# Another order of the first attention groups and of the first expert's tokens, filler products for TensorE, and fourteen subtractions on another engine

## The chip, the core and the metric

The program runs on one NeuronCore of a Trainium2 chip. Its engines are TensorE (PE; its weight loads are shown as PEld), VectorE (DVE), ScalarE (ACT), GpSimd (POOL) and SyncE (SP), which here issues the DMAs. Each engine works through its own instructions in order; semaphores tie them together. The metric is the device time of one launch in microseconds (us).

## What is computed

A block-windowed attention feeds a mixture of four experts without routing, and that feeds a gated MLP. Shapes: batch 2, 8 heads, 768 positions, head width 64, so 1536 tokens of width 512.

```python
k_sum = k.reshape(B, H, nb, 32, D).max(axis=3)       # 24 block maxima per head
v_sum = v.reshape(B, H, nb, 32, D).mean(axis=3)      # 24 block means per head
s_l = where(|i - j| < 16, scale * q @ k.T, -1e9)
s_s = scale * q @ k_sum.T + log(32)
a = softmax(concat([s_l, s_s]))
x = a @ concat([v, v_sum])                           # tokens x 512
p = domain_probs / (domain_probs.sum(-1) + 1e-9)
out = sum over e of p[:, e] * (relu(x @ w1[e]) @ w2[e])      # 512 -> 1024 -> 512, 4 experts
h = out @ w_in;  result = (h * sigmoid(1.702 * h)) @ w_out   # 512 -> 2048 -> 512
```

## The kernel before

**Numbers.** Matmuls take operands that are split into a high word (rounded to fp32r) and a low word (the rest, a subtraction). A product is a triple of matmuls: high by high, high by low, low by high. "Triple" below means these three.

**Attention groups.** A group is one batch, one head pair `hp` (two heads side by side on the 128 partitions) and four windows of 64 positions, 256 positions in all; there are 24 groups, numbered by the list `groups` (line 941). Batch 0 comes first: window start 0 for all four head pairs, then start 4, then start 8. A group passes through these steps, which the order below names by short words with the group's number: `Q`, `U` load queries and windowed values, `K`, `N` load keys and values of a head pair; `max` takes the 24 block maxima (DVE); for the first four groups `dl` and `dm` make the scores straight from keys and maxima (`direct_products`, L254), later ones copy windows (`win`, `wb`) and use `sc` (L247, 16 small matmuls); `msk` scales, masks and takes the row maximum (DVE, L276 and L281); `exp` is four exponentials with sums (ACT, L288) and adds 1e-9 to the sums (L292); `rec` inverts (DVE); `mul` scales (DVE `:v` or POOL `:g`, L300); `T` transposes (PE, L308); `aT` copies out (ACT, L314); `V` multiplies by the values (PE, L324); `xh` writes the high word of the result (ACT, L338), `low` the low word (DVE, L345). `mp`, `mq`, `mt`, `mc`, `mk`, `vb` make and spread the block means.

**First expert, batch 0.** `PIECES` (line 64) cuts its 768 tokens into pieces of 256 and 512, and the 8 blocks of 128 hidden columns make 16 units: 0 to 7 on the first 256 tokens, 8 to 15 on the other 512. Unit i has four first products, one for each head pair k (`f i.k`, L440; for units 0 to 3 they are called `e k.i` and have PSUM banks 0 to 3, later units share bank 4). Then `ga` applies relu and the gate (DVE, L392), `hh` makes the high word (ACT, L456), `hl` the low word (L398), and four second products `s i.d` (L478) add to the output banks. The gate values come from DRAM: `dp` loads, `gs`, `gr`, `gm` normalise, `ps` writes them to DRAM, `pb` reads them back spread over all partitions. The weights are loaded by `WA`, `WC`, split by `wh` (high, ACT) and `wl` (low, DVE or POOL).

**Pair 0.** The other experts and the MLP run in 44 pairs of hidden blocks by a seven-product scheme (`pair`); pair 0 is written out by hand at the end of the order. It needs sums over the tokens of batch 0: `wo` rebuilds x (DVE, L1033, four pieces), `d` are four differences (L490), `th`, `tl` their high and low words (L495, L498), `q` the seven products (L732), `mv`, `tt`, `tg`, `tr`, `tw` the way from them to the hidden words. `Sa`, `Ph`, `Pl` prepare the weights of pair 1.

**What sets the order.** The string `ORDER` lists all these steps; the loop under it records them in that order, so each engine gets its own steps in the order of the string. The tile pools and semaphores do the rest. Ahead of the string ten products of the identity with itself (L1139, "warm") keep PE working while the first loads land. The operands of the later stages (batch 1 of the experts, batch 0 and batch 1 of the MLP) come from `prepare`, which calls `operands` (L505): seven pieces, each a copy on ACT (L495) and a subtraction on POOL (L498, 128x768), and four differences on DVE. `spread` deals them out over pairs: the set "x" over pair 1 and pairs 9 to 11, the first set "y" over pairs 24 to 27, the second over pairs 29 to 31.

## Time and profile before

| what | value |
|---|---|
| median of 3 runs | 841.67 us (840.47 to 841.74) |
| the profiled execution's own time | 841.6 us |
| its span, first to last instruction | 839.8 us |
| PE busy | 824.9 us (98%) |
| DVE, ACT, POOL busy | 594.1, 418.5, 435.7 us |
| mean granted TensorE clock | 0.993 |

PE's busy time covers the modelled ends of pipelined matmuls, so a stretch that reads as busy can still run at half the clock or wait between instructions. The spacing of the starts tells more than the durations. From 152 us on the program is the regular sequence of pairs; what lies before is the stretch that the order string writes out.

### The profile page before, as it was taken

The page shows a single profiled execution, that of the slowest core. Times are in us where ns is not written, and L with a number is a line of the kernel's source. Part 1 is how long each engine was busy: PE and PEld are TensorE (multiplying, and loading weights), DVE is VectorE, ACT ScalarE, POOL GpSimd, SP SyncE. Part 2 cuts the span into 40 slices and gives each one's busy share as a digit, 9 for nine tenths or more (in the row PEclk, how much of TensorE's full clock was granted, in tenths as well). Part 3 has the DMA queues.
Part 4 walks back from the last instruction along what each step waited for, and adds up shares of the span by engine and source line. Part 5 has one row for each costly group of instructions (what it writes and reads, how often), then busy time and mean ns, then how long its engine had stood idle before and what let it go on. Part 6 is the DMA issues. An engine that isn't in the chain of part 4 may idle for free.

```text
span 839.8 us, 13639 instructions
## 1 busy us (share of the span) xinstructions
PE 824.9 (98%) x5114; PEld 747.3 (89%) x5114; DVE 594.1 (71%) x843; ACT 418.5 (50%) x972; POOL 435.7 (52%) x372
## 2 busy tenths in 40 slices
...
GB/s 289 203 174 186 114 65 211 115 218 285 218 289 206 162 228 185 223 285 290 233 289 280 255 278 101 54 73 150 151 204 178 170 199 201 247 167 116 171 78 76
DMA packets 48370, 159.93 MB, mean 190 GB/s; under 512 B 5424, under 2 KB 8752, under 8 KB 43184
## 3 DMA queue, kind: packets, MB, share of 16 engines
...
## 4 chain that ended last, share of the span: by engine, by line
PE 85%; DVE 8%; ACT 3%; issue 2%; DMA 2%; POOL 0%; DVEq 0%; POOLq 0%; ACTq 0%
PE o L856 25%; PE Y L732 19%; PE o L887 14%; PE X L732 5%; PE h L440 3%; PE o L478 3%; DVE S L602 2%; PE sc L247 2%; PE xo L324 2%; PE at L308 1%; DVE hid L398 1%; DVE g L774 1%; DMA k<-kq 1%; DVE x L1033 1%; PE warm L1139 1%
## 5 line engine op out<-in xcount | busy, mean ns | idle before, releaser
L856 PE MATMUL o<-hid,wB 128*128 128x512 f32 x1344 | 260.8, 336 | 0.7 <-POOL wB L642 0.6
L856 PEld LDWEIGHTS o<-hid,wB 128*128 128x128 f32 x1344 | 214.7, 188 | 22.0 <-POOL wB L642 1.0
L642 POOL TENSOR_TENSOR wB<-rawB,wB 128x512 fp32r<-128x512 f32 x88 | 122.9, 1407 | 158.0 <-ACT wB L638 148.7
L887 PE MATMUL o<-wB,hid 128*128 128x512 f32 x570 | 146.5, 394 | 0.3 <-ACT y L873 0.3
L784 ACT CAST hid<-g 128x384 fp32r<-128x384 f32 x172 | 88.3, 514 | 116.2 <-DVE g L774 84.8
L398 DVE TENSOR_TENSOR hid<-g,hid 128x384 fp32r<-128x384 f32 (+2 forms) x144 | 127.7, 899 | 6.8 <-ACT hid L784 5.3
L887 PEld LDWEIGHTS o<-wB,hid 128*128 128x128 f32 x570 | 105.7, 188 | 17.4 <-ACT y L873 0.7
L622 POOL TENSOR_TENSOR wA<-S,wA 128x512 fp32r<-128x512 f32 x48 | 72.6, 1513 | 37.0 <-ACT wA L618 26.8
L774 DVE SCALAR_TENSOR_TENSOR g<-g,pb 128x384 f32<-128x384 f32 x81 | 85.0, 1050 | 1.0
L622 POOL TENSOR_TENSOR wA<-rawA,wA 128x512 fp32r<-128x512 f32 (+1 forms) x48 | 56.5, 1179 | 48.7 <-ACT wA L618 39.8
L398 POOL TENSOR_TENSOR hid<-g,hid 128x384 fp32r<-128x384 f32 (+2 forms) x48 | 53.7, 1118 | 51.6 <-ACT hid L784 27.7
L732 PE MATMUL Y<-xt,wA 128*128 128x384 f32 x324 | 64.9, 334 | 0.0
L732 PE MATMUL Y<-xh,wA 128*128 128x384 f32 x216 | 63.7, 335 | 0.1
L797 ACT COPY prq<-Y 128x384 f32<-128x384 f32 x43 | 20.7, 480 | 80.7 <-PE Y L732 69.9
L695 POOL TENSOR_TENSOR arena<-arena 128x512 int32<-128x512 int32 x32 | 37.2, 1162 | 45.0 <-DVE arena L690 12.1
L732 PEld LDWEIGHTS Y<-xt,wA 128*128 128x128 f32 x324 | 53.9, 188 | 2.2
L638 ACT CAST wB<-rawB 128x512 fp32r<-128x512 f32 x88 | 52.5, 618 | 0.7 <-DMA rawB<-wts 0.7
L812 ACT COPY prq<-Y 128x384 f32<-128x384 f32 x43 | 20.6, 480 | 58.6 <-PE Y L732 58.6
L781 ACT ACTIVATE sg<-g 128x384 f32<-128x384 f32 x48 | 25.3, 527 | 48.5 <-DVE g L789 48.5
L782 DVE TENSOR_TENSOR g<-g,sg 128x384 f32<-128x384 f32 x48 | 37.0, 770 | 14.9 <-ACT sg L781 13.5
L789 DVE TENSOR_TENSOR g<-X,prq 128x384 f32<-128x384 f32 x43 | 23.8, 554 | 33.2 <-PE X L732 21.1
L602 DVE TENSOR_TENSOR S<-rawA 128x256 f32<-128x256 f32 x48 | 45.7, 954 | 1.8 <-POOL wA L622 1.8
...
## 6 DMA issues: line engine op xcount, KB each, us to landing
...
```

The lines of the kernel that those rows point to most:

```text
L398: engine.tensor_tensor(out=hl, in0=g, in1=hh.bitcast(F32), op=ALU.subtract)
L602: nc.vector.tensor_tensor(out=t[:, o], in0=a, in1=b, op=op)
L622: engine.tensor_tensor(out=lo, in0=x, in1=hi.bitcast(F32), op=ALU.subtract)
L638: nc.scalar.copy(wB[j][:, 0, f], rawB[j][:, f])
L642: nc.gpsimd.tensor_tensor(out=lo, in0=rawB[j][:, f], in1=hi.bitcast(F32), op=ALU.subtract)
L695: nc.gpsimd.tensor_tensor(out=o, in0=hi, in1=lo, op=ALU.add)
L732: nc.tensor.matmul(ps[:, 0:HS], ws[w], xs[x][:, k], start=(fresh and k == 0 and m == 0), stop=(k == 1 and m == 2), skip_group_check=True,)
L774: nc.vector.scalar_tensor_tensor(out=g, in0=g, scalar=0.0, in1=pbs[ph, s][:, tok], op0=ALU.max, op1=ALU.mult)
L782: nc.vector.tensor_tensor(out=g, in0=c, in1=sg, op=ALU.mult)
L784: heads.append(lambda: nc.scalar.copy(hh, g))
L856: nc.tensor.matmul(o, wB[j][:, w, f, c], tiles[f][:, x, t], start=fr, stop=last, skip_group_check=True,)
L887: nc.tensor.matmul(o, tiles[f][:, x, c], wB[j][:, w, f], start=(new and f == 1 and m == 0), stop=(stops and f == 0 and m == 2),)
```

## The change

1. The list of groups runs by head pair: for each head pair of batch 0 windows 0 and 4, then window 8 for all four. The first four groups, which make scores straight from the keys, are now head pairs 0 and 1 with two windows each. Their scores use PSUM banks 5, 3, 2 and 5 in place of bank 5 alone. The block means are spread by POOL for all groups but the first; for the other opening groups ACT writes one window's means and POOL three.
2. The first expert's tokens are cut into 512 and 256. The early first products of units 0 to 3 may be made by halves of 256 tokens (`e k.i.h`): for head pairs 0 and 1 by halves (16 triples of 256), for 2 and 3 whole (8 triples of 512).
3. Six warming products in place of ten, and twelve more (`x1`, on bank 1, which nothing else uses yet) between the first groups: six, two and four.
4. Adding 1e-9 to the sums is a step of its own, on ACT for 13 groups and on POOL for 11.
5. `prepare` takes an engine: the subtractions of the set "x" and of the first set "y" are on DVE, the second set "y" stays on POOL.
6. The order string is new throughout.

```diff
--- before.py
+++ after.py
@@ -36,6 +36,7 @@
 GQ = GW * WIN
 LAG = 2
 EARLY = 4
+WARM = 6
 NEG = -1.0e9
 
 TINY = math.ldexp(1.0 + 1.0 / 8, (897 << 20 >> 23) - 127)
@@ -61,7 +62,7 @@
         return psum.tile([P, 512], F32, tag=f"bank{n}", name=name)
 
 
-    PIECES = [(0, GQ), (GQ, S - GQ)]
+    PIECES = [(0, 2 * GQ), (2 * GQ, S - 2 * GQ)]
     units = [(c0, n, f) for c0, n in PIECES for f in range(NF)]
     N = len(units)
 
@@ -109,8 +110,8 @@
 
     def load_q(g):
         b, hp, w0 = g
-        if b == 0 and w0 == 0 and hp < HP - 1:
-            t = q_home[:, hp]
+        if g in groups[: HP - 1]:
+            t = q_home[:, groups.index(g)]
         else:
             t = att.tile([P, GQ], F32, tag="q", bufs=4, name="q{}{}{}".format(*g))
         c = PAD + w0 * WIN
@@ -227,9 +228,12 @@
         nc.tensor.transpose(ps[0:KA], vsum[hp % 2], ident)
 
     def spread_means(g):
-        nc.gpsimd.tensor_copy(
-            vs[g][KW:KA], vms[g[:2]][KW:KA].unsqueeze(1).to_broadcast([NB, GW, P])
-        )
+        b, hp, w0 = g
+        if b or w0 == 2 * GW:
+            out, means = vs[g][KW:KA], vms[b, hp][KW:KA]
+        else:
+            out, means = vs[g][KW:KA, 0 if w0 else 1 :], v_homes[hp // 2][KW:KA, hp % 2, 0]
+        nc.gpsimd.tensor_copy(out, means.unsqueeze(1).to_broadcast(list(out.shape)))
 
     def means_tile(b, hp):
         vms[b, hp] = att.tile([P, P], F32, tag="vm", bufs=4, name=f"vm{b}{hp}")
@@ -255,7 +259,7 @@
         b, hp, w0 = g
         k, q = kts[b, hp], qs[g]
         if c0 == 0:
-            scs[g] = bank(5, f"sc{b}{hp}{w0}")
+            scs[g] = bank({1: 3, 2: 2}.get(groups.index(g), 5), f"sc{b}{hp}{w0}")
         ps = scs[g]
         for j in range(GW):
             w = (w0 + j) * WIN
@@ -289,8 +293,16 @@
                 s[:, j, :], s[:, j, :], AF.Exp, bias=nm[:, j : j + 1], scale=1.0,
                 accum_out=sm[:, j : j + 1],
             )
-        nc.scalar.activation(sm, sm, AF.Copy, bias=1e-9)
         st[g] = (s, sm)
+
+    def tiny_term(g, e):
+        sm = st[g][1]
+        if e == "s":
+            nc.scalar.activation(sm, sm, AF.Copy, bias=1e-9)
+        else:
+            engines[e].tensor_scalar(
+                out=sm, in0=sm, scalar1=1.0, scalar2=1e-9, op0=ALU.mult, op1=ALU.add
+            )
 
     def inverses(g):
         nc.vector.reciprocal(out=st[g][1], in_=st[g][1])
@@ -432,14 +444,16 @@
             hid[i] = bank(hidden_bank(i), f"h{i}")
         products(i, k)
 
-    def products(i, k):
+    def products(i, k, h=None):
         c0, n, f = units[i]
-        c, x = slice(k * P, (k + 1) * P), slice(c0, c0 + n)
+        y0, y1 = (0, n) if h is None else (h * GQ, (h + 1) * GQ)
+        c, x = slice(k * P, (k + 1) * P), slice(c0 + y0, c0 + y1)
         whi, wlo = part_of(f, A, 0), part_of(f, A, 1)
         for m, (wt, xx) in enumerate(((whi, xh[0]), (whi, xl[0]), (wlo, xh[0]))):
             nc.tensor.matmul(
-                hid[i][:, 0:n], wt[:, c], xx[:, k, x],
-                start=(k == 0 and m == 0), stop=(k == KC - 1 and m == 2),
+                hid[i][:, y0:y1], wt[:, c], xx[:, k, x],
+                start=(k == 0 and m == 0 and not h), stop=(k == KC - 1 and m == 2),
+                skip_group_check=i < EARLY,
             )
 
     def gated_hidden(i):
@@ -448,10 +462,10 @@
 
     def hidden_high(i):
         c0, n, f = units[i]
-        if c0 or i % 2 == 0:
+        if c0 == 0 or i % 2 == 0:
             shared["h"] = hid_tile((0, 1, 0)[shared["n"] % 3], f"hid{i}")
             shared["n"] += 1
-        c = slice(0, n) if c0 or i % 2 == 0 else slice(n, 2 * n)
+        c = slice(0, n) if c0 == 0 or i % 2 == 0 else slice(n, 2 * n)
         g, hh, hl = hid[i], shared["h"][:, 0, c], shared["h"][:, 1, c]
         nc.scalar.copy(hh, g)
         hid[i] = (hh, hl)
@@ -463,20 +477,20 @@
     def emptied(d, c0, n):
         if "acc" not in xf:
             xf["acc"] = slot("acc", [P, KC, S], F32, "acc0")
-        nc.scalar.copy(xf["acc"][:, d, c0 : c0 + n], part["ps"][d][:, 0:n])
+        nc.scalar.copy(xf["acc"][:, d, c0 : c0 + n], part[c0, d][:, 0:n])
 
     def seconds(i):
         c0, n, f = units[i]
 
         def one(d):
-            if f == 0 and d == 0:
-                part["ps"] = [bank(k, f"o{c0}{k}") for k in range(KC)]
+            if f == 0:
+                part[c0, d] = bank(d, f"o{c0}{d}")
             c = slice(d * P, (d + 1) * P)
             hh, hl = hid[i]
             whi, wlo = part_of(f, C, 0)[:, c], part_of(f, C, 1)[:, c]
             for m, (a, b) in enumerate(((whi, hh), (whi, hl), (wlo, hh))):
                 nc.tensor.matmul(
-                    part["ps"][d][:, 0:n], a, b,
+                    part[c0, d][:, 0:n], a, b,
                     start=(f == 0 and m == 0), stop=(f == NF - 1 and m == 2),
                 )
 
@@ -502,11 +516,11 @@
         ((1, 1), (1, 1), (0, 0)), ((1, 0), (1, 0), (1, 1)),
     )
 
-    def operands(s, src):
+    def operands(s, src, engine=nc.gpsimd):
         def parts(hi, lo, x):
             def act():
                 rounded(hi(), x())
-                rest_of(lo(), x(), hi(), nc.gpsimd)
+                rest_of(lo(), x(), hi(), engine)
 
             return act
 
@@ -938,7 +952,8 @@
         ]
 
 
-    groups = [(0, hp, w0) for w0 in range(0, NW, GW) for hp in range(HP)]
+    groups = [(0, hp, w0) for hp in range(HP) for w0 in (0, GW)]
+    groups += [(0, hp, 2 * GW) for hp in range(HP)]
     groups += [(1, hp, 0) for hp in range(HP)]
     groups += [(1, hp, w0) for hp in range(HP) for w0 in range(GW, NW, GW)]
     NG = len(groups)
@@ -948,45 +963,46 @@
 
 
     ORDER = """
-    K0 Q0 N0 max0 dl0 K1 win4 dm0 mp0 msk0 Q1 Q2 WA1 max1 exp0 dl1 K2 mq0 dm1 mt0 msk1 U0 whA1:s
-    N1 wlA1:g max2 dl2 exp1 N2 rec0 dm2 mul0:v mp1 msk2 K3 T0 mc0 aT0 rec1 Q3 exp2 mul1:v V0 U1
...
+    Q0 K0 dl0 max0 WA1 Q1 N0 dm0 whA1:s dl1 msk0 wlA1:g K1 dm1 x1 x1 x1 x1 x1 x1 msk1 exp0 Q2 mp0 Q3
+    WA2 mq0 dl2 WA0 exp1 ad0:g mt0 rec0 dl3 x1 x1 max1 mul0:g U0 K2 whA2:s T0 ad1:g rec1 whA0:s dm2
...
     """
 
     xh[0] = slot("xh0", [P, KC, S], F32R, "xh0")
@@ -1004,7 +1020,10 @@
 
     def means_first(hp):
         ps = mean_ps.pop(hp)[KW:KA, 0:P]
-        nc.scalar.mul(vs[0, hp, 0][KW:KA], ps.unsqueeze(1).to_broadcast([NB, GW, P]), 1.0 / BLK)
+        n = 1 if hp else GW
+        nc.scalar.mul(
+            vs[0, hp, 0][KW:KA, 0:n], ps.unsqueeze(1).to_broadcast([NB, n, P]), 1.0 / BLK
+        )
 
     def means_kept(n):
         b, hp = openers[n]
@@ -1014,10 +1033,10 @@
             v = v_homes[hp // 2][KW:KA, hp % 2, 0]
             nc.gpsimd.tensor_copy(means_tile(b, hp), v)
 
-    def early(k, i):
-        if k == 0:
+    def early(k, i, h=None):
+        if k == 0 and not h:
             hid[i] = bank(hidden_bank(i), f"h{i}")
-        products(i, k)
+        products(i, k, h)
 
     def second(i, d):
         if i not in seconds_of:
@@ -1114,7 +1133,7 @@
         "whA": lambda e, n: high(n, A, copies[e]), "whC": lambda e, n: high(n, C, copies[e]),
         "wlA": lambda e, n: remainder(n, A, engines[e]),
         "wlC": lambda e, n: remainder(n, C, engines[e]),
-        "e": lambda e, k, i: early(k, i), "f": lambda e, i, k: first(i, k),
+        "e": lambda e, *n: early(*n), "x": lambda e, n: spin(n), "ad": lambda e, n: tiny_term(G[n], e), "f": lambda e, i, k: first(i, k),
         "ga": lambda e, n: gated_hidden(n),
         "hh": lambda e, n: lows.__setitem__(n, hidden_high(n)),
         "hl": lambda e, n: lows.pop(n)(engines[e]),
@@ -1134,9 +1153,15 @@
         "tl": lambda e, n: rest_of(operand(n)[2], operand(n)[1], operand(n)[0], engines[e]),
     }
 
-    ps = bank(3, "warm")
-    for _ in range(10):
-        nc.tensor.matmul(ps[:, 0:P], ident, ident, start=True, stop=True)
+    warm = {}
+
+    def spin(n):
+        if n not in warm:
+            warm[n] = bank(n, "warm")
+        nc.tensor.matmul(warm[n][:, 0:P], ident, ident, start=True, stop=True)
+
+    for _ in range(WARM):
+        spin(0)
     for word in ORDER.split():
         word, _, e = word.partition(":")
         name = word.rstrip("0123456789.")
@@ -1147,7 +1172,7 @@
     def late_tile(tag, shape, dt, name):
         return late[0].tile(shape, dt, tag=tag, name=name)
 
-    def prepare(s, name):
+    def prepare(s, name, engine=nc.gpsimd):
         def begin():
             make = (slot, late_tile)[s]
             xh[s] = make(f"xh{s}", [P, KC, S], F32R, f"{name}h{s}")
@@ -1160,7 +1185,7 @@
                 xt[s] = late_tile("xt0", [P, 2, 3, 2, HS], F32R, f"{name}t{s}")
 
         src = {"x": lambda: xf[1], "y": lambda: xf["y1"] if s else xf["acc"]}[name]
-        return [begin, begin_t] + operands(s, src)
+        return [begin, begin_t] + operands(s, src, engine)
 
     extra = [[] for _ in pairs]
 
@@ -1186,14 +1211,14 @@
         spread([lazy(n, k) for n in range(n0, n1) for k in range(4)], j0, j1)
 
     converts(0, SPLIT64, 2, S1 - 3)
-    acts_x = prepare(1, "x")
+    acts_x = prepare(1, "x", nc.vector)
     spread(acts_x[:1] + acts_x[2:5], 1, 2)
     spread(acts_x[1:2] + acts_x[5:], S1 - 3, S1)
     extra[S1 + 1].append(
         open_arena(lambda: late_tile("xt0", [P, 9 * DM], I32, "arena1"), SPLIT64, ND)
     )
     converts(SPLIT64, ND, S1 + 1, P0 - 4)
-    spread(prepare(0, "y"), P0 - 4, P0)
+    spread(prepare(0, "y", nc.vector), P0 - 4, P0)
     spread(prepare(1, "y"), P0 + 1, P0 + 4)
 
     for j in range(1, NPAIR):
```

PE at its start, before (`sc` are scores, `mean` block means, `at` transposes, `xo` value products, `h` first products):

```order
L1139 MATMUL warm<-ident 128x128 x10
L264 MATMUL sc_134<-k_128,q_home 64x96 x8
L264 MATMUL sc_134<-ks_132,q_home 64x24 x8
L264 MATMUL sc_171<-k_143,q_home 64x96 x8
L264 MATMUL sc_171<-ks_163,q_home 64x24 x8
L227 MATMUL mean_191<-ident,vsum_106 120x128
L264 MATMUL sc_203<-k_180,q_home 64x96 x8
L264 MATMUL sc_203<-ks_201,q_home 64x24 x8
L308 MATMUL at_236<-ident,s_156 120x128 x4
L324 MATMUL xo_254<-aT_242,v_home_94 64x64 x8
```

PE at its start, in the changed kernel:

```order
L1161 MATMUL warm<-ident 128x128 x6
L268 MATMUL sc_127<-k_125,q_home 64x96 x8
L268 MATMUL sc_127<-ks_136,q_home 64x24 x8
L268 MATMUL sc_150<-k_125,q_home 64x96 x8
L268 MATMUL sc_150<-ks_136,q_home 64x24 x8
L1161 MATMUL warm<-ident 128x128 x6
L268 MATMUL sc_196<-k_164,q_home 64x96 x8
L228 MATMUL mean_212<-ident,vsum_106 120x128
L268 MATMUL sc_215<-k_164,q_192 64x96 x8
L1161 MATMUL warm<-ident 128x128 x2
L320 MATMUL at_233<-ident,s_159 120x128 x4
```

The first two groups now share one tile of keys, both are scored before a second one is needed, and the fillers stand between the scores and the first transposes.

DVE at the end of the order string, before (`x` is the rebuilt input, `xt` and `xl` low words for pair 0, `hid` low words of the hidden units, `g` gated values):

```order
L398 TENSOR_TENSOR hid_1671<-g,hid_1671 128x512
L392 SCALAR_TENSOR_TENSOR g<-h_1782,pb_456 128x512
L1033 TENSOR_TENSOR x_1877<-xh_115,xl_116 128x768 x4
L398 TENSOR_TENSOR hid_1855<-g,hid_1855 128x512
L490 TENSOR_TENSOR x_1877<-x_1877 128x2x384 x4
L498 TENSOR_TENSOR xt_1876<-x_1877,xt_1876 128x768
L498 TENSOR_TENSOR xl_116<-x_1877,xh_115 128x2x384
```

And in the changed kernel:

```order
L404 SCALAR_TENSOR_TENSOR g<-h_1829,pb_693 128x256
L410 TENSOR_TENSOR hid_1769<-g,hid_1769 128x256
L410 TENSOR_TENSOR hid_1888<-g,hid_1888 128x256
L1052 TENSOR_TENSOR x_1904<-xh_115,xl_116 128x768 x4
L504 TENSOR_TENSOR x_1904<-x_1904 128x2x384 x3
L512 TENSOR_TENSOR xt_1903<-x_1904,xt_1903 128x768
L404 SCALAR_TENSOR_TENSOR g<-h_1895,pb_693 128x256
L512 TENSOR_TENSOR xt_1903<-x_1904,xt_1903 128x768
```

The chain for pair 0 is about the same, but the units beside it are 256 wide: on PE, 17 triples of 128x256, `q0` and `q1` stand between the last value products (`V23`) and `q2`, which reads the second `xt`; before there were 16 triples of 128x512, `q0` and `q1`.

## Rows read from the trace of the kernel before

**Rows 1.** Windows: us; busy PE, PEld, DVE, ACT, POOL (instructions); PEclk, DMA, GB/s.
```profile
5.80:12.50 6.70, 4.02 (x82) 3.29 (x81) 4.85 (x8) 3.21 (x15) 2.39 (x3) 1.00 1.03 367
12.50:19.40 6.90, 5.78 (x59) 4.82 (x61) 5.57 (x11) 5.50 (x20) 3.42 (x4) 0.51 1.03 300
...
34.60:127.30 92.70, 90.39 (x948) 74.16 (x948) 68.94 (x136) 67.70 (x255) 49.13 (x68) 0.98 0.47 143
127.30:152.20 24.90, 24.62 (x118) 21.03 (x117) 21.71 (x25) 9.50 (x18) 8.59 (x6) 1.00 0.51 190
520.00:560.00 40.00, 39.93 (x231) 37.11 (x230) 38.29 (x43) 18.38 (x36) 27.49 (x20) 1.00 0.22 67
```
**Rows 2.** Chain that ended last: start us, us, what (matmuls counted singly).
```profile
1.36 4.56 PE warm L1139 x20
5.92 1.26 PE sc L264 x32
...
27.24 2.24 DMA pscr<-dp
...
29.50 4.11 DMA pb<-pscr
...
41.01 1.08 PE o L478 x9
42.09 0.97 PE sc L247 x16
...
48.75 0.44 PE at L308 x4
49.19 0.61 PE xo L324 x16
...
55.96 6.52 DMA k<-kq
...
64.87 1.63 ACT s L288 x8
...
150.09 2.08 PE o L478 x9
```
**Rows 3.** Timeline of the opening: start us, us, engine, line, op, tiles, [idle before].
```profile
3.89 0.95 DVE L194 TENSOR_REDUCE ks<-k 128x24 f32<-128x768 f32 x1 [2.81 <-DMA k<-kq]
...
17.36 0.35 ACT L338 CAST xh<-xo 128x256 fp32r<-128x256 f32 x1
17.96 0.59 ACT L314 COPY aT<-at 120x512 f32<-120x512 f32 x1 [0.24 <-PE at L308]
...
19.91 0.39 PE L440 MATMUL h<-xh,w0A 128*128 128x256 f32 x1
...
34.62 0.96 PE L478 MATMUL o<-hid,w0B 128*128 128x256 f32 x3 [1.90 <-ACT hid L456]
```
**Rows 4.** Timeline of the end of the order string, DVE and PE.
```profile
127.52 5.99 DVE L1033 TENSOR_TENSOR x<-xh,xl 128x768 f32<-128x768 f32 x4 [1.46 <-ACT wA L618]
...
135.13 4.47 DVE L490 TENSOR_TENSOR x<-x 128x768 f32<-128x768 f32 x4
...
140.89 1.34 PE L732 MATMUL pair0y<-xt,wA 128*128 128x384 f32 x6 [0.28 <-ACT prq L1065]
```
**Rows 5.** Groups by line and shape: xcount | busy us, mean ns | idle before.
```profile
L498 DVE TENSOR_TENSOR xt<-x,xt 128x768 fp32r<-128x768 f32 x3 | 2.9, 951 | 0.0
...
L300 POOL TENSOR_TENSOR s<-s,sm 128x480 f32<-128x480 f32 x9 | 9.0, 1000 | 12.5 <-DVE sm L296 12.5
...
L498 POOL TENSOR_TENSOR yl<-acc,yh 128x768 fp32r<-128x768 f32 x4 | 8.6, 2156 | 0.0
```
**Rows 6.** Timeline of pair 1's end, DVE and POOL.
```profile
171.27 1.55 DVE L398 TENSOR_TENSOR hid<-g,hid 128x384 fp32r<-128x384 f32 x1
...
177.51 0.55 DVE L398 TENSOR_TENSOR hid<-g,hid 128x384 fp32r<-128x384 f32 x1
...
170.23 2.17 POOL L498 TENSOR_TENSOR xl<-x,xh 128x768 fp32r<-128x768 f32 x1
```

More of the change, by code (lines that the diff above doesn't have):

```diff
@@ L981, in attention_moe_mlp @@
-    sc23 vb19 ga12 exp22 vb20 T21 msk23 vb21 V19 vb22 f13.0 hl10:v exp23 s9.3 rec22 mul22:v
-    f13.1 U23 s10.0 wBh1 rec23 mul23:v hh12 f13.2 wBl1 xh19 aT21 f13.3 wBh0 hl12:v V20 wBl0 ga13
-    T22 xh20 V21 pl3 f14.0 xh21 aT22 f14.1 Sa0 rb1 s10.1 Sa1 Sa3 f14.2 Sa2 vb23 T23 hl11:v V22
-    f14.3 xh22 aT23 s10.2 Ph2 ga14 Ph0 Pl2 s10.3 Ph1 Pl0 Ph3 V23 s11.0 xh23 hh13 Pl1 f15.0 s11.1
-    Pl3 f15.1 s11.2 wo0:v f15.2 wo2:v s11.3 wo3:v s12.0 hh14 wo1:v f15.3 hl13:v s12.1 d0 s12.2
-    d1 th0 s12.3 q0 d2 th2 d3 s13.0 th1 q1 tl1:v th4 mv0 s13.1 tl4:v s13.2 hl14:g tt0 s13.3 tg0
@@ L987, in attention_moe_mlp @@
-    q2 tl2:v tr0 s14.0 tw0:v mv1 tl0:v s14.1 pl2 q3 ga15 hh15 s14.2 mv2 hl15:g q4 ra2 s14.3 tt1
-    q5 tg1 kp tr1 s15.0 tg2 q6 tw1:v tr2 eu0 tw2:v s15.1 tt2 s15.2 tg3 tr3 s15.3 eu1 tw3:v eu2
-    eu3
+    Q0 K0 dl0 max0 WA1 Q1 N0 dm0 whA1:s dl1 msk0 wlA1:g K1 dm1 x1 x1 x1 x1 x1 x1 msk1 exp0 Q2 mp0 Q3
+    WA2 mq0 dl2 WA0 exp1 ad0:g mt0 rec0 dl3 x1 x1 max1 mul0:g U0 K2 whA2:s T0 ad1:g rec1 whA0:s dm2
+    mul1:v U1 dm3 aT0 wlA2:g msk2 N1 mc0 T1 V0 x1 x1 x1 x1 aT1 wlA0:g max2 WA3 xh0 exp2 Q4 low0 vb1
@@ new lines, in attention_moe_mlp @@
+    msk3 Q5 e0.2.0 U2 e0.0.0 mp1 e0.1.0 N2 whA3:s V1 win4 mq1 wb4 xh1 ad2:g sc4 win5 K3 rec2 wlA3:v
+    mt1 mul2:g low1 e0.3.0 Q6 mc1 msk4 exp3 e0.1.1 Q7 mp2 e0.3.1 e0.0.1 Q8 max3 T2 N3 wb5 vb2 ad3:s
+    sc5 aT2 win6 rec3 wb6 exp4 U3 mul3:g e0.2.1 msk5 WA4 V2 U4 T3 win7 ad4:s xh2 sc6 U5 rec4 wb7 mq2
+    aT3 mul4:g U6 low2 exp5 mt2 msk6 WA5 e1.1.0 mp3 e1.3.0 e1.2.0 U7 e1.0.0 vb3 mq3 ad5:s U8 whA4:s
+    T4 rec5 mk0 mul5:v mc2 V3 aT4 wlA4:v mt3 xh3 sc7 vb4 exp6 low3 mk2 vb5 T5 msk7 U9 V4 dp ad6:s
@@ new lines, in attention_moe_mlp @@
+    e1.1.1 WC1 xh4 rec6 mc3 e1.0.1 mul6:v aT5 e1.2.1 WC0 low4 exp7 e1.3.1 whA5:v f4.0 wlA5:v V5 vb6
+    ad7:s T6 mk3 xh5 vb7 low5 f4.1 aT6 vb8 rec7 e2.2 mul7:v win8 e2.3 wb8 win9 e2.1 wb9 gs V6 gr T7
+    gm xh6 sc8 low6 aT7 whC1:s V7 msk8 whC0:s ps wlC1:g pb e2.0 xh7 f4.2 low7 exp8 wlC0:g Q9 e3.0
+    Q10 Q11 e3.1 WA6 ad8:g e3.2 win10 rec8 WC3 ga0 wb10 mul8:g e3.3 ga1 hh0 WC2 sc9 hl0:v hh1 M2
+    whA6:s T8 hl1:v whC3:s s0.0 wlA6:g msk9 WA7 s0.1 WC5 wlC3:g ga2 f4.3 M0 ga3 hh2 s0.2 whC2:s ga4
@@ new lines, in attention_moe_mlp @@
+    Y0 s0.3 aT8 wlC2:v whA7:s f5.0 mk1 max14 exp9 WC4 vb9 s1.0 wlA7:v Y2 f5.1 whC5:v s1.1 ad9:s
+    wlC5:g Y1 rec9 f5.2 mul9:v s1.2 hl2:g f5.3 s1.3 mp4 ga5 V8 max12 T9 sc10 mq4 aT9 whC4:v xh8 hh3
+    win11 s2.0 wb11 win12 hh4 f6.0 wb12 hl3:g s2.1 M3 f6.1 hl4:v s2.2 wlC4:g low8 WC7 msk10 f6.2 M1
+    s2.3 f6.3 WC6 hh5 s3.0 ga6 Q12 Q13 mt4 whC7:v sc11 U10 mk4 exp10 wlC7:g U11 f7.0 U12 win13 s3.1
+    max13 ad10:s f7.1 rec10 msk11 wb13 mul10:g s3.2 f7.2 whC6:v exp11 s3.3 wlC6:g T10 sc12 mp6
+    ad11:s hh6 rec11 aT10 V9 win14 msk12 wb14 s4.0 xh9 mul11:g s4.1 low9 vb10 exp12 U13 vb11 sc13
```

49 lines of the change are left out of this document (21 added, 28 removed).

## The prediction, made before the changed kernel ran

> **What bounds the kernel now.** PE bounds it, so only time in which PE does nothing useful can be won. I read the windows first, to see where that is. From 152 us on there is next to none: even at 520 to 560 us, where DVE is busy for 38.29 of 40 us, PE is busy for 39.93 [rows 1]. What can be won lies before. There I don't trust busy time, since half clock and modelled ends hide in it, and count work instead. A triple of 256 columns takes 0.36 us (1.08 for three), one of 512 takes 0.69 (2.08 for three), scores 0.97, transposes 0.44, value products 0.61, a direct group of scores 1.26 [rows 2]; a mean I put at 0.2, an estimate.
>
> PE's work ahead of the first second product (`s0.0`): 4 direct groups 5.0, 2 scores 1.9, 4 transposes 1.8, 4 value products 2.4, 4 means 0.8, 19 triples of 256 6.8: 18.7 us. It begins at 34.6 us [rows 3]. So **15.9 us of the opening are lost**. The chain shows to what: warming products until 5.92, a little past the landing of the first keys at 3.89 [rows 2, 3]; then the latency of each group; the first useful product at 19.91 [rows 3]; half clock, 0.51 granted from 12.5 to 19.4 [rows 1]; last the gates' way through DRAM, 2.24 and 4.11 us [rows 2], for which PE waits 1.90 [rows 3].
>
> Between 34.6 and 127.3 PE is idle for 2.3 us and the clock is 0.98, which is 3.7 us at half speed, 1.9 us of work [rows 1]. The idle part is the keys of batch 1: their load takes 6.52 us and the exponentials behind it stand in the chain [rows 2]. At the end, 127.3 to 152.2, only 0.3 us is idle [rows 1, 4].
>
> **The opening.** The sum is made against the profiled 841.6 us, as good as the median 841.67. With six warming products, each 0.46 (4.56 for ten, two matmuls each), PE is free at 4.1. Queries now go ahead of the first keys, by one issue, so the keys land near 4.3. Two groups then need only one load of keys. By hand: maxima until 5.3, scores until 6.2 (at half clock as in the slow stretch), mask and row maximum 1.3, exponentials 1.63 until 9.3, the sums' term and `rec` behind the means' work on DVE until 10.2, `mul` on POOL 1.0 [rows 5]: `T0` at 11.5, the result's high word at 14.4 in place of 17.36 [rows 3], the first useful product at 15.4 in place of 19.91. From there PE's queue is mostly fed, because sixteen half triples can be taken as soon as one window of a head pair is done; ACT is the longest, at 1.63 + 0.59 + 0.35 us per group [rows 2, 3] plus the weights' copies. That brings the eighth group's scaling to 34.5, the gates' normalisation behind it on DVE and POOL to 37.5, the 6.4 us through DRAM to 43.9, gate, high and low word to 46.3.
>
> What PE has to do until then is more: 5.0 direct, 6 scores 5.8, 9 transposes 4.0, 8 value products 4.9, means 0.8, 16 triples of 256 5.8, 11 of 512 7.6: 33.9. Lost: 46.3 - 33.9 = 12.4, against 15.9: **-3.5 us**. PE would get to `s0.0` near 44.3, so it waits 2 us there again. The ends: -6 if the gates come in time, 0 if the clock falls in the opening as it did before. Twelve fillers cost nothing as long as they stand before `T0` and the first triple, whose inputs are late anyway; without that cover they are 12 x 0.2 = 2.6 us.
>
> **The middle.** The wait for batch 1's keys should go, since they are issued earlier against PE's work and the units beside them are twice as long: **-1.9** of the 2.3 idle (ends -2.3 and 0). The half clock followed the wait for the gates; I leave that wait, so I leave its price too: 0 (ends -1.9 and 0). Groups 19 to 23 now stand close together, with as much ACT work as PE work around them: **+0.4** (ends 0 and +1.5). Half triples: two of 0.36 for one of 0.69, eight times: **+0.2**.
>
> **The end of the order string.** Here the change costs. DVE's chain for pair 0 starts after the last value products: four pieces 5.99, four differences 4.47 [rows 4], low words 0.95 each [rows 5]. Until `q2` PE had 16 triples of 512 and 2 x 1.05: 13.1 us. Now it has 17 of 256, 6.1 + 2.1 = 8.2 us. The chain: two low words of units 0.7, four pieces at 1.0 to 1.1 (1.5 before, beside POOL's subtractions, which now mostly come later) 4.2, three differences 2.9, low, gate, low 2.3: 10.1. PE waits **+2.0** at `q2`, less the 0.3 it waits now. After it `q5` needs `tl4`, which stands behind a difference and two weight sums: **+0.6**. POOL then has pair 1's low words of weights late, behind ACT's copies: **+0.5** (ends 0 and +0.9). Sum +2.8 (ends 0 and +7, with pieces at 1.5 each and pair 1's second weights, whose buffer now comes free last, not yet landed).
>
> **The two sets.** Fourteen subtractions go from POOL, 2.16 each, to DVE, 0.95 each [rows 5]. DVE has little room: 1.7 us in 40 in pairs 24 to 27 [rows 1], where seven of them, 6.7 us, are added. But POOL's work slows DVE's: the same subtraction takes 0.55 us alone and 1.55 beside POOL's 2.17 us [rows 6], 0.46 us for each us of POOL. Seven fewer take 15.1 us off POOL and 6.9 off DVE. The two cancel, and POOL is relieved: **-0.4** (ends -1 and +4.5). The Trainium skill, SBUF — State Buffer, section Who interferes with whom, says that VectorE with two SBUF inputs and a GpSimd instruction that reads SBUF share a read interface, and that the second to start is fully blocked. By that rule the seven would free up to 15.1 us of VectorE, and the sum would still move by no more than the 0.1 us that PE idles there; the trace shows 1.0 of 2.17 us, less than full blocking.
>
> **Sum:** -3.5 - 1.9 + 0.4 + 0.2 + 2.8 - 0.4 = -2.4: 839.2 us.
>
> **Rivals.** *All of it pays.* The gates come in time (-2.0), no half clock (-1.9), and DVE's chain is covered because PE lags (the +2.8 gone): 832.5. For it: no long gap of PE is left in the opening; against: the DRAM way of 6.4 us is untouched. The Trainium skill, TensorE: Matmul & The Clock Gate, section What's actually happening, says that the default clock is the low one and that PE's activity releases it. By that rule the fillers count as activity and would keep 2.4 GHz granted; here PE was busy for 4.02 of the 6.70 us before the clock fell to 0.51 [rows 1], so activity alone did not hold it.
> *The fillers don't hold the clock.* It falls to half in the opening once more: 6.9 us with PE busy for 5.8 cost 2.9 [rows 1], the opening is worth 0.6 and the sum is +0.5: 842.1, no change.
> *Slower: DVE becomes the bound.* Pairs 24 to 27 last some 64 us (687.6 us after 152.2 for 43 pairs), and at the rate of 1.7 in 40 [rows 1] DVE is idle for 2.7 of them. If POOL's work slows DVE by less than 0.26 us per us, the seven subtractions (6.7 - 15.1 x 0.26 = 2.8) use that up, and PE waits. With no relief at all that is 4.0 there, and 0.5 more in pair 1: +4.5 in place of -0.4, 844.1. Against it stands the 0.46 measured; the end of the string at its upper bound (+7) gives the same side, 843.4.
>
> **Chances and range.** Forecast 0.46, all pays 0.22, fillers fail 0.16, slower 0.16. About 0.2% (1.7 us) is what a measurement tells from no change: 840.0 to 843.4. The forecast's own spread (837 to 841.5) lies for three quarters below 840.0, so faster has 0.34 + 0.22 = 0.56; same 0.12 + 0.12 = 0.24; slower 0.20. The range, 833.5 to 843.5, leaves out the lowest part of the second case and the upper half of the last.
>
> **What would show it.** Right: first useful product near 15.4, `s0.0` near 46 with about 2 us of wait on the gates, no wait behind batch 1's keys, some 2 us of PE idle before the third product of pair 0, DVE's 128x768 subtractions near 1 us and no new idle of PE at 520 to 585. Wrong: a clock of half speed between 6 and 30 us, `s0.0` later than 49, no wait at `q2`, or PE waiting for DVE's low words in pairs 24 to 28.

## The result, and the profile after

The changed kernel takes **834.16 us** (median of 4 runs, 832.16 to 835.48) against 841.39 (4 runs): ratio 0.991 [0.9892, 0.9928]. Run again beside eleven runs of the kernel before it took 831.74 (831.29 to 833.44), ratio 0.9885 [0.9869, 0.9902]. The forecast was 839.2 with a range of 833.5 to 843.5: faster, as said, but by 7 to 10 us where 2.4 was said. The profiled execution took 833.45 us.

The head of its page, and its windows (columns as in [rows 1]):

```profile
span 831.7 us, 13705 instructions
...
PE 823.6 (99%) x5154; PEld 748.8 (90%) x5154; DVE 577.7 (69%) x852; ACT 413.8 (50%) x957; POOL 419.5 (50%) x381
```
```profile
5.80:12.50 6.70, 6.70 (x83) 6.29 (x81) 4.15 (x8) 3.71 (x18) 3.60 (x5) 1.00 1.02 327
12.50:19.40 6.90, 6.90 (x111) 6.14 (x113) 5.05 (x10) 4.72 (x15) 4.96 (x6) 1.00 0.93 297
46.40:127.30 80.90, 80.58 (x810) 67.36 (x809) 55.93 (x109) 52.50 (x190) 48.26 (x66) 1.00 0.43 134
127.30:143.20 15.90, 15.58 (x115) 15.11 (x110) 14.85 (x22) 7.66 (x17) 4.03 (x3) 1.00 0.41 150
```

PE is busy for 80.58 of 80.90 us between `s0.0` and the last value products, with the clock full; before it was 90.39 of 92.70 at 0.98 [rows 1]. The 1.00 of the first window needs care: the trace has no clock record ahead of the first rise, which stands at 10.8 us here, and the products before it run at the low level (see the ten warming products below).

To see where the time came from, the timeline of PE at six landmarks: first useful product, `s0.0`, the last value products (`V23`), the first product of pair 1, and one product of the regular pairs early and one late. First after, then the four of before that aren't shown yet:

```profile
17.43 0.36 PE L453 MATMUL h<-xh,w0A 128*128 128x256 f32 x1
...
46.49 0.89 PE L492 MATMUL o<-hid,w0B 128*128 128x512 f32 x2
...
126.86 0.69 PE L336 MATMUL xo<-aT,vw 120*64 120x64 f32 x16
...
143.23 0.34 PE L746 MATMUL Y<-xh,wA 128*128 128x384 f32 x1
...
213.97 1.20 PE L746 MATMUL Y<-xt,wA 128*128 128x384 f32 x6
...
637.49 1.23 PE L746 MATMUL Y<-yt,wA 128*128 128x384 f32 x6
```
```profile
126.64 0.69 PE L324 MATMUL xo<-aT,vw 120*64 120x64 f32 x16
...
152.01 0.33 PE L732 MATMUL Y<-xh,wA 128*128 128x384 f32 x1
...
221.30 1.20 PE L732 MATMUL Y<-xt,wA 128*128 128x384 f32 x6
...
645.74 1.23 PE L732 MATMUL Y<-yt,wA 128*128 128x384 f32 x6
```

The last three landmarks compare directly: the lead over the kernel before is 8.8 us at the start of pair 1, 7.3 at 214 us and 8.2 at 637. The first three stand behind different amounts of work, so lost time is counted as the forecast did, elapsed less useful. At `s0.0`: 46.5 - 33.9 = 12.6, before 15.9. From there to `V23`, with the forecast's duration of each group: before 92.0 - 82.3 = 9.7, after 80.4 - 76.6 = 3.8.

| stretch | forecast | measured |
|---|---|---|
| opening, to `s0.0` | -3.5 | -3.3 |
| middle, `s0.0` to `V23` | -1.9 + 0.4 + 0.2 = -1.3 | **-5.9** |
| end of the order string and pair 1, to 214 us | +2.8 | +1.9 (lead 9.2, then 8.8 and 7.3) |
| two sets on DVE, as far as between 214 and 637 us | -0.4 | -0.9 |
| sum | -2.4 | -8.2 |

The waits of PE say the same. Before, then after (engine and line, what for, us in total, times, longest):

```profile
PE at L308 <- DVE s L300: 2.1, 3, 1.0
PE o L478 <- ACT hid L456: 1.9, 1, 1.9
...
PE sc L264 <- DMA q_home<-kq: 1.1, 1, 1.1
PE sc L264 <- DVE ks L194: 1.1, 2, 0.7
```
```profile
PE o L870 <- POOL wB L656: 0.7, 1, 0.7
PE X31b L746 <- DVE g L803: 0.4, 1, 0.4
PE Y L746 <- ACT prq L821: 0.4, 1, 0.4
...
PE o L492 <- DVE g L404: 0.3, 1, 0.3
PE pair0y L746 <- DVE xt L512: 0.3, 1, 0.3
```

Apart from the start of the warming products (1.4 us in both), the four waits that led the list are gone. The first of them is 0.45 us at 14.0 and the two at 65.7 and 68.4 us that belong to the keys of batch 1. Of what PE still waits for, 0.3 and 0.4 us stand in pairs 0 and 1; the 0.7 at 352 us and the 0.4 in pair 31 the kernel before has too (0.6 and 0.4).

### The profile page after: what moved, and what is told of

Same layout as the page of the kernel before. It is cut to its first block, busy times and chain, and to the rows that moved or that the text cites. A ratio compares the mean times of both kernels' runs of the same rounds, so it can differ in the third digit from the quotient of the medians.

```text
span 831.7 us, 13705 instructions
## 1 busy us (share of the span) xinstructions
PE 823.6 (99%) x5154; PEld 748.8 (90%) x5154; DVE 577.7 (69%) x852; ACT 413.8 (50%) x957; POOL 419.5 (50%) x381
## 4 chain that ended last, share of the span: by engine, by line
PE 89%; DVE 5%; ACT 2%; DMA 1%; issue 1%; POOL 1%; SPq 0%; DVEq 0%; ACTq 0%; POOLq 0%
PE o L870 27%; PE Y L746 20%; PE o L901 14%; PE X L746 5%; PE o L492 3%; PE h L453 2%; PE sc L251 2%; PE xo L336 1%; PE at L320 1%; DVE S L616 1%; PE sc L268 1%; DMA pb<-pscr 1%; DVE hid L410 1%; ACT s L292 1%; PE warm L1161 0%
## 5 line engine op out<-in xcount | busy, mean ns | idle before, releaser
L410 DVE TENSOR_TENSOR hid<-g,hid 128x384 fp32r<-128x384 f32 (+2 forms) x142 | 118.9, 851 | 7.6 <-ACT hid L798 5.6
L410 POOL TENSOR_TENSOR hid<-g,hid 128x384 fp32r<-128x384 f32 (+2 forms) x50 | 55.9, 1120 | 50.6 <-ACT hid L798 27.7
L636 POOL TENSOR_TENSOR wA<-rawA,wA 128x256 fp32r<-128x256 f32 (+1 forms) x48 | 56.4, 1177 | 48.6 <-ACT wA L632 39.1
L788 DVE SCALAR_TENSOR_TENSOR g<-g,pb 128x384 f32<-128x384 f32 x81 | 77.6, 958 | 1.0
L746 PE MATMUL Y<-xt,wA 128*128 128x384 f32 x324 | 65.2, 335 | 0.5 <-ACT prq L821 0.4
L746 PE MATMUL Y<-xh,wA 128*128 128x384 f32 x216 | 63.5, 334 | 0.0
L746 PEld LDWEIGHTS Y<-xt,wA 128*128 128x128 f32 x324 | 53.9, 188 | 3.2 <-ACT prq L821 0.7
L803 DVE TENSOR_TENSOR g<-X,prq 128x384 f32<-128x384 f32 x43 | 23.8, 555 | 32.9 <-PE X L746 21.3
```

The lines of the kernel that those rows point to most:

```text
L410: engine.tensor_tensor(out=hl, in0=g, in1=hh.bitcast(F32), op=ALU.subtract)
L636: engine.tensor_tensor(out=lo, in0=x, in1=hi.bitcast(F32), op=ALU.subtract)
L746: nc.tensor.matmul(ps[:, 0:HS], ws[w], xs[x][:, k], start=(fresh and k == 0 and m == 0), stop=(k == 1 and m == 2), skip_group_check=True,)
L788: nc.vector.scalar_tensor_tensor(out=g, in0=g, scalar=0.0, in1=pbs[ph, s][:, tok], op0=ALU.max, op1=ALU.mult)
```

## The experiments

The question was what carries the gain: the fillers, the half triples, the pieces, the gates, or the keys of batch 1. All kernels compute everything.

### Without the fillers

```diff
- K1 dm1 x1 x1 x1 x1 x1 x1 msk1 ... dl3 x1 x1 max1 ... V0 x1 x1 x1 x1 aT1
+ K1 dm1 msk1 ... dl3 max1 ... V0 aT1
```

> The changed kernel without its twelve fillers between the first groups (the six warming products stay). Theory: the fillers close the gaps in which the clock fell before; without them PE is idle for some 5 us between 8 and 18 us, the clock falls to half once in the first 30 us and the opening loses 1.5 to 3 us: 835.7 to 837.2. Rival: the new order alone keeps PE fed, the fillers stand only where PE waits anyway, and the time is that of the changed kernel within 0.5 us, 834.

Measured: 832.69 us (829.97 to 835.91), 0.9904 [0.988, 0.9929]. The theory fell: the gain doesn't hang on the fillers.

### The fillers in the kernel before

```diff
- dl0 K1 win4 dm0 mp0 ... dl1 K2 mq0 dm1 mt0 msk1 ... dl2 exp1 N2 rec0 dm2 mul0:v ... T0 mc0
+ dl0 K1 win4 dm0 x1 x1 x1 x1 mp0 ... dl1 x1 x1 K2 mq0 dm1 mt0 x1 x1 msk1 ... dl2 x1 x1 exp1 N2 rec0 dm2 x1 mul0:v ... T0 x1 mc0
```

> The kernel before with the twelve filler products of the change in PE's first gaps (4 after the second group's scores, 2, 2, 2, 1 and 1 behind later ones). Theory, from the run without fillers, where the clock held all the same: the fillers do little, and the opening is set by the other engines' latency; the clock may hold at 12.5 to 19.4 us, but the first useful product comes at most 1 us earlier: 840.5 to 842 us. Rival, the opening of the changed kernel is faster because the clock holds: 838 to 839.5 us.

Measured: 839.57 us (836.57 to 841.0), 0.9976 [0.9962, 0.999]; the profiled execution, 836.99, is one of its fastest. The windows of the kernel before at 36.4 us, then of this one at the two places where the clock had been at half:

```profile
36.40:39.80 3.40, 3.40 (x19) 3.40 (x18) 3.37 (x6) 3.01 (x12) 2.71 (x5) 0.50 1.08 317
```
```profile
12.50:19.40 6.90, 6.05 (x91) 5.00 (x91) 6.80 (x14) 6.25 (x21) 3.54 (x6) 1.00 1.08 307
36.40:39.80 3.40, 3.40 (x38) 3.11 (x37) 3.33 (x8) 2.92 (x14) 2.11 (x4) 1.00 0.45 135
```

The second stretch runs at the full clock, though PE waited 1.9 us for the gates here too (`PE o L478 <- ACT hid L456: 1.9, 1, 1.9`). So in this execution that wait did not bring the half clock, and the half clock is worth 1.7 us (half of 3.4). It is not the common execution: the three of the ten runs with a mean clock of at least 0.999 took 836.6 to 837.6 us, the seven with 0.997 or 0.998 took 838.5 to 841.0. Nor do the falls always come without fillers: of 62 runs of the kernel before, timed beside these experiments, three had 0.998 and took 838.5 to 839.8, the others 0.988 to 0.996. The median lies between theory and rival: here fillers help, since the order leaves gaps.

### Keys of batch 1 out of DVE's way

```diff
- sc11 low8 aT9 max15 exp10 ... exp13 s7.2 mp7
+ sc11 low8 aT9 exp10 ... exp13 s7.2 max15 mp7
```

> The kernel before with one step of DVE moved: the block maxima of the last head pair of batch 1 (max15) stand some 60 words later in the order. Before, PE waited about 2.2 us between 64 and 69 us while DVE stood at those maxima for a load of keys that takes 6.52 us. Theory, the wait is DVE's queue held up by one step whose input is late: it goes and nothing takes its place, 839.5 to 840.0 us, and between 60 and 72 us PE loses less than 0.5 us. Rival, that stretch is short of DMA bandwidth: the wait moves to the next load that PE, DVE or ACT needs, 841 to 842.5 us.

Measured: 841.03 us, 0.9997 [0.9986, 1.0009]: no change, the rival. DVE's timeline shows two waits, both for batch 1's loads, where the kernel before waited for the fourth keys:

```profile
60.71 0.95 DVE L194 TENSOR_REDUCE ks<-k 128x24 f32<-128x768 f32 x1 [1.30 <-DMA k<-kq]
...
70.67 1.01 DVE L218 TENSOR_REDUCE vsum<-vT 128x24 f32<-128x384 f32 x2 [1.70 <-POOL vT L188]
```

The second is the values of the same batch, which POOL passes on. PE then waits 1.8 us for DVE, up to 73.4 us. One step can't be moved out of the way, since all of batch 1's loads are wanted in a short time. That is what the change alters: DVE's maxima of batch 1, before and after:

```profile
52.57 0.94 DVE L194 TENSOR_REDUCE ks<-k 128x24 f32<-128x768 f32 x1
...
62.57 0.95 DVE L194 TENSOR_REDUCE ks<-k 128x24 f32<-128x768 f32 x1 [1.55 <-DMA k<-kq]
```
```profile
51.31 0.94 DVE L195 TENSOR_REDUCE ks<-k 128x24 f32<-128x768 f32 x1
...
66.89 0.94 DVE L195 TENSOR_REDUCE ks<-k 128x24 f32<-128x768 f32 x1
...
82.16 0.94 DVE L195 TENSOR_REDUCE ks<-k 128x24 f32<-128x768 f32 x1
```

Four maxima within 10 us before, the same four within 31 us now, and none waits. Between them PE has first-expert units of 512 tokens.

### The pieces back to 256 and 512

```diff
- PIECES = [(0, 2 * GQ), (2 * GQ, S - 2 * GQ)]
+ PIECES = [(0, GQ), (GQ, S - GQ)]
```

and the early products without their second halves, so that units 0 to 7 have 256 tokens again; order of the groups, fillers and sets stay.

> The changed kernel with the tokens cut into 256 and 512 as before; of the early half triples only the first halves are left, the order is else the same. Theory: PE has 6.5 us less work before the first second product, the gates still come at 44.7, so PE waits there for 5 to 6 us and the clock falls: +5 to +7, 839 to 841. Rival: the groups by head pair carry the gain and the pieces are worth 1 us or less: 835.

Measured: 846.58 us (844.62 to 848.03), 1.0062 [1.0042, 1.0081], slower than before. Its waits, and two windows:

```profile
PE at L320 <- POOL s L312: 4.0, 3, 3.4
PE sc L251 <- DVE g L404: 2.6, 1, 2.6
```
```profile
44.00:51.00 7.00, 6.34 (x38) 6.06 (x39) 4.97 (x11) 3.49 (x7) 3.75 (x4) 0.51 1.01 352
51.00:68.00 17.00, 12.46 (x124) 11.19 (x124) 12.37 (x23) 6.62 (x27) 8.79 (x12) 1.00 0.64 208
```

PE is idle for 4.5 of the second window's 17 us, and the clock is at half twice, from 44 to 51 us and again behind the second window (68.0 to 71.4). The theory had the direction and half of the size. The piece size moves 12.4 us in this order, which was written for the long units; the kernel before has the short ones and is faster than this run.

### Whole triples in place of half ones

```diff
- e0.2.0 low1 e0.0.0 ... e0.1.1 ... e0.2.1
+ low1 ... e0.1 ... e0.2
```

The early products of head pairs 0 and 1 are eight triples of 512, each at its second half's place.

> The changed kernel with the sixteen early half triples joined to eight whole ones of 512 tokens, each at the place of its second half in the order. Theory, the forecast's step: the halves are what keeps PE fed from 15 us on; without them PE waits ahead of its transposes for about the work that is moved back, 2 to 3 us between 13 and 25 us, and the first second product stands 1.5 to 3 us later than 46.5: 836 to 838 us. Rival 1: the order of the groups alone keeps PE fed and only the 0.2 us for split triples changes: 833.5 to 834.5. Rival 2: with the gap the clock falls to half as it did before, and this costs another 2 us: 838 to 840.

Measured: 833.44 us (831.92 to 835.96), 0.9889 [0.9866, 0.9912]: rival 1. In the trace `s0.0` stands at 48.46, 2.0 us later than after, but the lead at 221 us is 6.2 in place of 7.3, 1.1 us less. By these traces the halves are worth about one us; the medians don't show it (833.44 here, 834.16 with the halves).

### The gates' steps ahead, in the kernel before

```diff
- low1 dp e0.2 ... xh2 gs whC1:s ... whA4:s gr e2.2 WA7 gm aT3 ... win5 ps wb5 f4.0 pb
+ Q3 dp ... mp2 gs ... mt1 gr ... mul2:g gm ... N3 ps pb
```

> The kernel before with the gates' steps (load, normalisation, write to DRAM and read back) moved ahead in the order by some 3 us of work; all else stays. Theory, PE's wait of 1.90 us at the first second product goes and with it the half clock that followed at 36.4 to 39.8 us (3.4 us at half speed, 1.7 of work): 838 to 838.6 us, and the granted clock is full from 19.4 us on. Rival 1, the clock's fall comes from somewhere else than that wait: 839.8 to 840.3. Rival 2, the hidden units behind the gates are late as well, since ACT has no room: PE waits as before, 841 to 842.

Measured: 843.27 us (841.37 to 844.67), 1.0019 [1.0007, 1.0031]: none of the three fits. The wait at the first second product is gone, but PE waits 1.6 us for a head pair's values (`PE xo L324 <- DMA v_home<-vw: 1.7`) and 1.6 for the means on ACT, both before 33 us, probably since the gates' work and its DMA had pushed these back; no row shows this. `s0.0` stands at 38.88, 4.3 us later. The half clock came twice too, at 0.50 between 12.5 and 19.4 us and 0.88 over 30 to 44, the second time without a wait for the gates ahead of it. So that wait was neither what bounds the opening alone nor what the half clock needs.

### The sets back on POOL

```diff
- acts_x = prepare(1, "x", nc.vector)
+ acts_x = prepare(1, "x")
- spread(prepare(0, "y", nc.vector), P0 - 4, P0)
+ spread(prepare(0, "y"), P0 - 4, P0)
```

> The changed kernel with both sets of subtractions back on POOL. Theory: the two engines' costs nearly cancel and PE shows only the small waits of the kernel before again (0.3 near 178, 0.35 near 546, 0.5 near 592): +0.5, 834.7, ends 0 and +1. Rival: DVE pays for the sets in the changed kernel, and it gets faster by 1 us or more without them.

Measured: 833.03 us (832.39 to 835.72), 0.9909 [0.9891, 0.9928]. This is 1.1 us less than the changed kernel's first median, as the rival has it, and 1.3 more than its second (831.74), so the medians decide nothing and the traces have to. Here PE waits 1.2 us in pair 2 (`PE X2b L746 <- DVE g L803: 1.2, 1, 1.2`), which the changed kernel doesn't, and its lead over before stays at 9.4 and 9.3 between the two regular landmarks, where the changed kernel gains 0.9. At the start of pair 1 (140.39 here) the lead was 11.6; it loses 2.2 up to 214 us, the changed kernel 1.5. Together the two sets are worth some 1.7 us in this order, by these two executions. The windows of 500 to 600 us, of before, of this one and of the changed kernel:

```profile
500.00:600.00 100.00, 99.59 (x567) 92.40 (x566) 91.82 (x104) 54.09 (x108) 73.34 (x50) 1.00 0.33 108
```
```profile
500.00:600.00 100.00, 99.59 (x560) 92.21 (x559) 89.25 (x102) 54.95 (x109) 72.44 (x50) 1.00 0.31 105
```
```profile
500.00:600.00 100.00, 100.00 (x567) 93.12 (x566) 83.81 (x111) 55.48 (x108) 57.60 (x43) 1.00 0.32 106
```

With seven subtractions more (0.95 each, 6.7 us) DVE is busy for 5.4 us less than with the sets on POOL. So 14.8 us off POOL take 12.1 off DVE: about 0.8 us per us, not the forecast's 0.46. This run's opening was luckier (`s0.0` at 44.45 for 46.49), which hides the gain in the total (next).

### Ten warming products, and the changed kernel once more

```diff
- WARM = 6
+ WARM = 10
```

> The changed kernel with ten warming products in place of six. Theory: with ten the clock rises at 5.7 us as in the kernel before and not at 10.8, which gives back about 1.5 us of half speed work, and the first scores start 1.3 us later; the chain through DVE and ACT decides, so the two cancel: -0.5 to +0.5, 833.7 to 834.7. Rival: the clock decides the opening, and the time falls by 1.5.

> The changed kernel once more, unedited, on the same chip as the run below. Theory: the time of one and the same kernel is spread over some 3 us by when the clock first rises (in the first profile at 10.8 us, in the run with the sets on POOL, whose opening is the same, at 4.3): where the profile shows the rise ahead of 6 us, the first second product stands near 44.5 us, where it shows it near 10.8, near 46.5; the median stays at 832.5 to 835 us. Rival: the spread comes from the loads, and the first second product is at the same place whenever the clock rises.

Ten: 832.08 us (830.57 to 833.36), 0.9892 [0.9874, 0.991], no cost seen. That is below the theory's 833.7 and near the rival's number, but the unedited kernel again took 831.74, below the median expected, so the two can't be told apart. With ten the clock rose at 7.3 us in the profile, and `s0.0` stood at 45.21. PE's timeline at the first scores, in the first profile and in the second:

```profile
4.53 1.55 PE L268 MATMUL sc<-k,q_home 64*64 64x96 f32 x16 [0.24 <-DMA k<-kq]
5.84 1.03 PE L268 MATMUL sc<-ks,q_home 64*64 64x24 f32 x16
6.65 1.56 PE L268 MATMUL sc<-k,q_home 64*64 64x96 f32 x16
7.96 1.03 PE L268 MATMUL sc<-ks,q_home 64*64 64x24 f32 x16
8.93 2.47 PE L1161 MATMUL warm<-ident 128*128 128x128 f32 x12
11.32 0.88 PE L268 MATMUL sc<-k,q_home 64*64 64x96 f32 x16
```
```profile
4.74 1.25 PE L268 MATMUL sc<-k,q_home 64*64 64x96 f32 x16 [0.45 <-DMA k<-kq]
5.81 0.61 PE L268 MATMUL sc<-ks,q_home 64*64 64x24 f32 x16
6.25 0.87 PE L268 MATMUL sc<-k,q_home 64*64 64x96 f32 x16
6.93 0.61 PE L268 MATMUL sc<-ks,q_home 64*64 64x24 f32 x16
7.47 1.60 PE L1161 MATMUL warm<-ident 128*128 128x128 f32 x12
```

The same sixteen matmuls take 1.56 us in one and 0.87 in the other: the first execution runs at the low level until about 11 us, the second until about 5.5. `s0.0` follows: 46.49 and 45.05 (44.45 in the run with the sets on POOL, at full speed from 4.3). The theory holds, with 1.4 us for 2 expected.

### Looking for a better one

Without fillers, second set "y" on DVE too; the first version also moved pair 1's weights (`wBh0 wBl0 rb1`) up behind `mv1`, the second did not.

```diff
- spread(prepare(1, "y"), P0 + 1, P0 + 4)
+ spread(prepare(1, "y", nc.vector), P0 + 1, P0 + 4)
```

> The changed kernel without the twelve fillers, with the subtractions of the second set y on VectorE too, and with the low words of pair 1's first weights (wBh0, wBl0) and their buffer's load (rb1) some 15 words earlier. Theory: PE's waits of 0.57 us near 627 us and of 0.56 us at 150 us go; against the run without fillers (832.69 us) that is 831.5 to 832.2 us. Rival: VectorE has no room for seven more subtractions near pairs 29 to 31 and PE waits for it there, 833 to 836 us.

> The changed kernel without the twelve fillers and with the subtractions of the second set y on VectorE as well; nothing else moved. Theory: PE's wait of 0.57 us near 627 us goes, and the order of pair 0 and 1 stays as in the run without fillers: 831.8 to 832.4 us. Rival: VectorE has no room near pairs 29 to 31: 833 us or more. The run must also show no wait of 2.4 us near 137 us, which came from the moved weights of pair 1 alone.

> The changed kernel without fillers and with the second set y on VectorE, beside the changed kernel itself on the same chip. Theory: faster than it by 1.5 to 4 us (830 to 832 us). Rival: the difference seen so far was between chips and between moments of the clock's rise: within 1 us of it.

The first: 831.68 us (831.14 to 837.46), 0.9902 [0.9875, 0.9928], within the theory's range, but not for its reason. The moved weights made a new wait, in PE's timeline:

```profile
140.22 0.44 PE L746 MATMUL pair0y<-xl,wA 128*128 128x384 f32 x1 [2.37 <-DVE xl L512]
```

That low word took 2.01 us beside POOL's moved work; alone it takes 0.95. The second: 830.04 us (829.43 to 835.32), 0.9869 [0.984, 0.9897], without that wait, and its lead over before grows from 10.5 us at 283 to 12.1 at 706. But beside the changed kernel on one chip it took 830.93 (829.12 to 835.39), 0.9883 [0.986, 0.9906], against 831.74, 0.9885: no difference shown. From `s0.0` to the end its trace is 1.0 us shorter (783.7 for 784.7); its opening is less sure (below).

## Why the prediction came out as it did

**Opening, -3.5: right in size, in part by luck.** `s0.0` at 46.49 for 46.3. Two steps under it were off and cancelled. The first useful product came at 17.43, not 15.4, because the low clock lasted to about 11 us; in the run at full speed from 4.3 it came at 15.34. So PE was some 2 us late itself, and the 2 us wait for the gates did not come, though the gates were no earlier than forecast. DVE's timeline, first gated values:

```profile
44.75 1.29 DVE L404 SCALAR_TENSOR_TENSOR g<-h,pb 128x512 f32<-128x512 f32 x2 [1.37 <-DMA pb<-pscr]
```

The forecast had the gates at 43.9. With the clock up at 5.5 the first gated values were made at 41.8, and PE was not held by them either. "Twelve fillers cost nothing" held at the full clock only: where it rose late, at 10.7 us, in the run without fillers too, `s0.0` stood at 45.19 without them and at 46.49 with them. (The 12 x 0.2 there makes 2.4, and six took 1.60 at the full clock.)

**Middle, -1.3: the mis-sized term.** "I leave that wait, so I leave its price too: 0" failed. The wait itself did not stay, and the half clock had its own price of 1.7, measured in the kernel before with fillers; with the gates ahead it came without that wait. The keys' wait went entirely, at the lower end of the forecast (its whole cost before, PE's three gaps from 64 to 68 us, was 2.2). The other 2.0 of the 5.9 were in no term, and only part of them can be placed. Some 0.4 is a wrong price: a group of transposes takes 0.53 us from start to start on average, not 0.44, and the new middle has five fewer (the opening has five more, so it won that much more than the table says). PE's two waits for means near 81 us, 0.4 in all, are gone. The rest lies in gaps too short for the list of waits; that PE now has a long unit at hand there is argued, not shown. And the +0.6 for close groups and half triples is not to be seen: from 50 us to `V23` the list has no wait of PE. The experiment with the pieces shows that in this order the stretch hangs on the 512 first tokens; the sum priced them with one number, the keys.

**End, +2.8: sign right, +1.9 measured, but in another place.** The chain at `q2`, in DVE's timeline and PE's:

```profile
127.91 3.57 DVE L1052 TENSOR_TENSOR x<-xh,xl 128x768 f32<-128x768 f32 x4
131.39 2.94 DVE L504 TENSOR_TENSOR x<-x 128x768 f32<-128x768 f32 x3
134.25 0.95 DVE L512 TENSOR_TENSOR xt<-x,xt 128x768 fp32r<-128x768 f32 x1
```
```profile
136.46 1.15 PE L746 MATMUL pair0y<-xt,wA 128*128 128x384 f32 x5 [0.32 <-DVE xt L512]
```

Pieces took 0.9 each with POOL idle, for the 1.05 taken; PE had 8.9 us of work up to the start of `q2`, not 8.2, since the sum left out `V23` itself; and PE waited 0.3 where +2.0 was forecast. For `q5` (+0.6) no wait is listed. So the whole end of the order string cost 0.4, lead 9.2 to 8.8. The other 1.5 went in pair 1, where the sum had +0.5 for late weights. There 0.4 is the wait for `prq`; what the rest waited for, in gaps below the list, is not shown.

**Sets, -0.4: right sign, some 1.7 by the traces (0.9 of it behind 214 us).** The price of POOL on DVE was twice the forecast's (0.8 for 0.46), so "the two cancel" was too dark, and DVE as a bound fell. The 0.46 was a misreading of [rows 6]. POOL's subtraction had run since 170.23 and ended at 172.40, DVE's began at 171.27: only 1.13 us of POOL's 2.17 lay beside it, and of these DVE lost 1.00. So the rows show nearly full blocking of the one that starts second, not "less than full blocking". The Trainium skill, SBUF — State Buffer, section Who interferes with whom, calls the port pair that the two engines share an exclusive lock; these rows agree with it.

**Rivals.** The time fell near "all of it pays" (832.5, chance 0.22), not near the forecast: no wait for the gates, no half clock; but the end's cost did not vanish as that case had it, the middle paid for it. That 834.16 lies within the range, by 0.7 us, is luck: the second median, 831.74, lies below it. "Fillers don't hold the clock" is not what happened, and holding it is not what the fillers were needed for in the typical run. They may insure: over all runs with fillers in the changed order (22, the one with the pieces turned round aside) the mean granted clock, which leaves out the time before the first rise, was never below 0.999, while in 4 of 24 without them it was 0.991 to 0.994, at 834.1 to 835.9 us. So few are a hint and no proof, and five more of the 24 took 835.2 to 837.5 us with a mean clock of 0.998 or more. The Trainium skill, TensorE: Matmul & The Clock Gate, section What's actually happening, has PE's activity release the clock; in every profile here the first products ran at the low level (six warming ones, twelve matmuls, took 2.93 us, where six fillers at the full clock took 1.60), which agrees.

**Open.** What decides when the clock first rises; where most of the middle's last 2.0 us and of pair 1's 1.5 come from; why some runs with the full clock take 835 us; and how the gain splits between the new group order and the pieces when both are changed: the pieces alone in the old order were not tried.
